# Three edits to a one-core attention and MoE kernel: where the last six output tiles are staged, how many rows eight heads' first scores contract over, and new numbers for the scheduler

## The chip, the cores and the metric

The kernel runs on one core of a Trainium2 chip (trn2). The metric is device time in microseconds (us) of one execution; a kernel's time is the median of several runs. The profile is one execution taken by the hardware profiler, and its span runs from the first to the last instruction.

## The reference

Three layers in float32, one after another. `q`, `k`, `v` are 4 x 8 x 576 x 64 (32 heads of 576 positions), `s` is 4 x 8 x 576, and `x` between the layers is 2304 x 512.

```python
def _attn_ref(q, k, v, s):
    scores = q @ k^T / sqrt(D)
    cum = np.cumsum(np.maximum(s, 0.0), axis=-1)
    bias = -(cum[:, :, :, None] - cum[:, :, None, :])
    scores = np.where(causal, -1e9, scores + np.minimum(bias, 0.0))
    attn = exp(scores - max);  attn = attn / (sum(attn) + 1e-09)
    return attn @ v

def _moe_ref(x, w1, w2, w3, w_out):      # 512 -> 1024 -> 1024 -> 512
    return ((x @ w1) * (x @ w2)) @ w3 @ w_out

def _moe2_ref(x, w_in, w_out):           # 512 -> 2048 -> 512
    h = x @ w_in
    return (h - np.tanh(h)) @ w_out
```

## The kernel before

**The stages.** (1) Attention, head by head, from 0 to about 309 us. (2) The products `x@w1` and `x@w2` and their elementwise product (`products`, matmuls at L826), mixed into the attention of later heads and going on after it. (3) `w3 @ w_out` as one matrix (L941 to L943), and the first MoE layer's output `x2` (L978 to L980). (4) The second MoE layer from about 533 us: three passes (`p`) of 768 tokens, in each eight steps (`fp`). A step forms seven matrix products per group of weights (`ws`, `x2b`, L1055), the gate `h - tanh(h)` on ACT and DVE into `gh` and `gl` (a high and a low part), and adds into six PSUM banks, each 128 tokens x 512, by three matmuls a bank and tile (L1095 to L1097). In the last step of a pass the six banks are complete; ACT copies each to SBUF and SP sends it to `out`.

**The order of the work** is made ahead of time by a list scheduler in the kernel (`Plan`). Each operation has a priority, a duration for each engine that may run it, and the buffers (or numbered parts of a buffer) that it reads and writes. The scheduler walks through modelled time and writes an instruction order for every engine; on the chip each engine keeps that order, and SP issues every DMA in its own. Priorities, and the biases by which an operation is given to ACT, DVE or POOL, come from the table `PARAM`. Where the scheduler sees PE idle in its first 66 us (`fu=66000`), it writes **dummy matmuls** (`filler`, L576) into the gap. They read a tile of zeros and nothing uses what they write. They are instructions like others: PE runs them in order whether or not work is ready.

**The first eight heads** (batch 0, `full`) compute a score tile in float32 by one matmul pair at L688 (head 0, `one`, by L686 and L695). There are five query tiles `t` of 64, 128, 128, 128 and 128 queries. The contraction has 64 rows of q and k, and five more, one for each query tile: on the query side 1 for the queries of that tile and 0 for others (`fix`), on the key side the cumulated bias relative to that tile's first position (`rel`). So the queries of tile `t` pick row 64+t. The tile `rqk` (two of them, for even and odd heads: `rqk_112` and `rqk_113` in the built program) holds both sides. Two DMAs fill its bias rows for a head: three rows for tiles 0 to 2 and two rows for tiles 3 and 4. Each score tile goes through a reduction on DVE (L705), an exponential on ACT (L711), transposes on PE against `ident` (L745), copies into `en`, and the matmul with v (L772). The first part of a `rel` row is ready only when the prefix scan over `s` is done on DVE.

**Conversions.** Weights come as 8-byte floats (`wraw`); `assemble` turns 512 columns into float32 in five steps (L515 or L516, then L517, L518, L520 and L522 on DVE), and a split into high and low parts follows. These run on ACT, DVE and POOL beside the attention.

**Output staging.** `osb_r` is a ring of two tiles of 128 x 512 (`nosb=2`). `tmp_r` is a ring of the seven tiles `cst` (three) and `asb` (four), which in stage 4 hold the step's intermediate products. In the last step of the last pass (`last`) every bank is copied in two halves of 256 columns.

```python
ob, t0, bk = osb_r.next(), p * 2 * XB + l * XB + n * P, bank[l * 3 + n]
for a, z in ((0, 256), (256, 512)) if last else ((0, 512),):
    ...
dma(lambda t0=t0: out[t0:t0 + P, :], lambda ob=ob: ob.t, P * DM * 4, [ob], [], 0)
```

Of the kernel before, what the change touches and what calls it, by code (L numbers as in the profile page):

```python
# [40 lines left out]
PARAM = dict(tail=346719, dsub2=2687.6, dcopy2=-363.2, dother2=15239, act2=-1777.4, pool2=4728.0, cs=1176.5, xs=-29.3, layw=10048, x2p=785.3, nwst=3, late=778.7,  # L41
             gate=4314.0, cst=6240.0, ramp0=1010.9, ramp1=-512.9, dsub=4382.6, dsub0=-2390.3, dcopy=-1480.1, dcopy0=-572.5, dother=1106.1, dother0=-2029.8,
             spi=2833.6, lay=0, layp=641747, layf=473733, dve0=1000.0, early=120052, raw0=0, rawp=-700.0, ng=8, nosb=2, cut=(), convq=2713.8, natb=8, nfull=8,
             wap=1402502, dve=1000.0, act=-598.5, pool=-114.4, sem=160.0, pesem=180.0, slow=1.1, convp=3444.2, npre=12, nbias=3, keep=0.5, ff=0.0, fu=66000,
             wlast=0, kbp=-210.2, qk=2491.2, kb=-1761.7, rv=-1179.0, st=83.8, fl=756.2, iv=1391.7, pv=-1105.8, ml=4388.9, bw=370.0, ntr=3, actb=1, actn=0,
             spp=3043.5, ne=2, nsb=2, ncf=5, outlag=187.2, o_qk=-577.9, o_kb=647.6, o_rv=179.7, o_iv=-2316.9, o_fl=-889.6, o_pv=-374.3, o_ml=-281.5, o_st=829.5,
             o_c0=-132.5, o_c1=211.6, o_c2=404.2, o_c3=3145.8, o_c4=-302.4, o_c5=1092.9, o_c6=-321.1, o_c7=-538.4, o_c8=-309.2, o_c9=568.4, o_c10=-644.8,
             o_c11=721.4, o_c12=620.5, o_c13=-386.2, o_c14=-1078.1, o_c15=-517.3, o_h0=-2746.5, o_h1=-2197.2, o_h2=507.3, o_h3=211.0, o_h4=-153.0, o_h5=1351.8,
             o_h6=-1038.9, o_h7=-501.6, o_h8=-600.0, o_h9=726.1, o_h10=-463.4, o_h11=308.3, o_h12=1634.4, o_h13=837.2, o_h14=-1715.4, o_h15=-171.3, o_h16=-831.4,
             o_h17=198.0, o_h18=-178.6, o_h19=1097.2, o_h20=517.6, o_h21=-1252.5, o_h22=177.5, o_h23=337.0, o_h24=-1368.9, o_h25=-531.3, o_h26=724.9, o_h27=-159.5,  # L50
             o_h28=2096.8, o_h29=-111.9, o_h30=-510.2, o_h31=-973.2)
# [289 lines left out]
def tile_kernel(ctx, tc, qk, v, s, w1, w2, w3t, w_out, w_in, w_out2, out):  # L341
# [108 lines left out]
    cst_r = abp.ring("cst", 3, [P, TB])  # L450
    asb_r = abp.ring("asb", 4, [P, TB])
# [4 lines left out]
    rqk = [att.buf(f"rqk{i}", [P, 2 * S], n=3) for i in range(2)]  # L456
# [50 lines left out]
    osb_r = p2.ring("osb", PARAM["nosb"], [P, DM], n=2)  # L507
# [90 lines left out]
    for e in e2[:1] + [None] + e2[1:]:  # L598
        if e is None:
            zero([lambda: ssum.t], [20], [ssum], -5, 1.0)  # L600
            for R in rqk:
                a = 0 if R is rqk[0] else S
                pl.op([("POOL", 1040.0 if a == 0 else 560.0, lambda R=R, a=a: nc.gpsimd.memset(R.t[D:D + 5, a:], 0.0))], w=[(R, (1, 2))], prio=-2300)
        else:
            zero([later(e, EOFF[0], EOFF[0] + D, low)], [D], [(e, 0)], -10 if e is e2[0] else 92, r=scan)
# [32 lines left out]
    def role(n, b):  # L638
        return PARAM[n] + (PARAM["o_" + n] if b == 0 else 0.0)

    def head(h, full, groups=(0, 1)):
# [32 lines left out]
        def softmax_tile(t):  # L674
            q0, q1 = QT[t]
            nq = q1 - q0
            p_ = pr + role("st", b) * t
            bi, bo = msk, (512 if nq < P else S) - q1
            pieces = [(0, q1)] if q1 <= 512 else [(0, HALF), (HALF, S)]
            for n, (k0, k1) in enumerate(pieces):  # L680
                bk = s_ring.next()

                def mm(bk=bk, k0=k0, k1=k1):
                    o_ = bk.t[:nq, :k1 - k0]
                    if one:
# [6 lines left out]
                if one:  # L692
# [3 lines left out]
                    pe(f_mm4(k1 - k0), mm, [R], [bk], p_ - 2000.0)  # L696
# [351 lines left out]
    def step(p, fp, pos, X, W):  # L1048
# [143 lines left out]
```

## Time and profile before

| what | us |
|---|---|
| median of 3 runs (lowest, highest) | 922.23 (921.72, 922.34) |
| the profiled execution, its whole time | 921.88 |
| its span | 920.2 |
| PE busy | 906.6 |
| DVE busy | 790.7 |
| ACT busy | 549.0 |
| POOL busy | 112.1 |

PE is TensorE's matmuls, DVE VectorE, ACT ScalarE, POOL GpSimd, SP the engine that issues the DMAs. Busy time of PE counts the dummy matmuls too, and it is modelled: matmuls are pipelined, so one that is listed with 0.39 us follows the one before after some 0.23 us. A window's idle time of an engine is its length less its busy time.

### The profile page before, as it was taken

Reading aid. Unit: us, or ns where it says so; the run is one execution under the profiler, and the core shown is the slowest. Engines: PE = TensorE matmul, PEld = TensorE weight load, DVE = VectorE, ACT = ScalarE, POOL = GpSimd, SP = SyncE. Lnnn points to the kernel's source line nnn. Section 1 sums busy time; section 2 is a strip of 40 time slices with the busy share of each in tenths; the row PEclk is TensorE's granted clock in tenths of the full one; section 3 lists DMA queues with packets and bytes.
Section 4 is the critical chain, followed back from the end, with each engine's and each line's share of the span. In section 5 each row is a group of like instructions: output and inputs, shape, how many; then the busy total and the mean of one; then the engine's idle time right before and its main releaser. Section 6 shows DMA issues by size and latency. Waiting matters only on the chain.

```text
span 920.2 us, 15850 instructions
## 1 busy us (share of the span) xinstructions
PE 906.6 (99%) x5174; PEld 790.6 (86%) x5174; DVE 790.7 (86%) x1884; ACT 549.0 (60%) x1292; POOL 112.1 (12%) x106
## 2 busy tenths in 40 slices
PE   9999999999999999999999989999999999999996
PEld 7777788888887888988999988989898998989885
DVE  8999999899999599989536999999998878787874
ACT  6998854343423013555446577777787667776765
POOL 1000044545442172000000000000000000000000
PEclk9999999999999999999999999999999999999998
DMA  7677766456565458898877595787977448644401
GB/s 222 202 227 194 217 203 213 130 186 212 177 220 161 154 179 279 275 296 282 270 231 236 189 306 173 255 275 236 387 236 260 116 117 304 200 116 123 115 12 69
DMA packets 102948, 189.94 MB, mean 206 GB/s; under 512 B 10594, under 2 KB 50690, under 8 KB 102867
## 3 DMA queue, kind: packets, MB, share of 16 engines
q1 hardware_dynamic: 102866, 188.94, 64.8%
q8 instruction: 41, 0.67, 0.3%
q14 instruction: 41, 0.33, 0.1%
HBM read 137.20 MB, written 48.01 MB: 201 GB/s over the span
## 4 chain that ended last, share of the span: by engine, by line
PE 89%; DVE 5%; DMA 3%; ACT 1%; issue 1%; SPq 0%; ACTq 0%; DVEq 0%
PE bank L826 21%; PE bank L1055 18%; PE bank L1096 7%; PE bank L1097 7%; PE bank L1095 7%; PE bank L745 5%; PE bank L772 5%; PE bank L979 2%; PE bank L978 2%; PE bank L980 2%; PE bank L690 2%; PE bank L688 2%; PE bank L691 2%; PE bank L941 2%; PE bank L942 2%; PE bank L943 2%
## 5 line engine op out<-in xcount | busy, mean ns | idle before, releaser
L1055 PE MATMUL bank<-x2b,ws 128*128 128x384 f32 x1008 | 192.9, 337 | 2.8 <-DMA ws<-ws_d 1.3
L1055 PEld LDWEIGHTS bank<-x2b,ws 128*128 128x128 f32 x1008 | 178.8, 188 | 12.1 <-DVE asb L1064 3.0
L711 ACT ACTIVATE e<-e,nmx 64x64 f32<-64x64 f32 (+4 forms) x160 | 89.1, 558 | 95.6 <-DVE nmx L705 95.0
L1097 PE MATMUL bank<-voh,gl 128*128 128x512 f32 x288 | 113.8, 395 | 0.0
L1096 PE MATMUL bank<-vol,gh 128*128 128x512 f32 x288 | 113.6, 394 | 0.0
L1095 PE MATMUL bank<-voh,gh 128*128 128x512 f32 x288 | 111.9, 389 | 0.0
L410 ACT ACTIVATE gh<-pg 128x384 fp32r<-128x384 f32 x96 | 50.0, 521 | 46.8 <-DVE pg L1087 46.5
L745 PE MATMUL bank<-ident,e 128*128 128x128 f32 (+1 forms) x480 | 75.4, 275 | 0.8 <-ACT e L711 0.7
L705 DVE CUSTOM_DVE_ANT_0 e<-bank,msk 64x64 f32<-64x64 f32 (+4 forms) x160 | 64.7, 420 | 4.5 <-PE bank L691 3.9
L1064 DVE TENSOR_TENSOR asb<-bank,cst 128x384 f32<-128x384 f32 x72 | 40.0, 555 | 33.2 <-PE bank L1055 32.8
L980 PE MATMUL bank<-xh,wal 128*128 128x384 f32 x192 | 64.1, 334 | 0.0
L978 PE MATMUL bank<-xh,wah 128*128 128x384 f32 x192 | 64.1, 334 | 0.0
L979 PE MATMUL bank<-xl,wah 128*128 128x384 f32 x192 | 64.1, 334 | 0.0
L1097 PEld LDWEIGHTS bank<-voh,gl 128*128 128x128 f32 x288 | 54.0, 187 | 11.5
L826 PE MATMUL bank<-xh,w2h 128*128 128x512 f32 (+1 forms) x160 | 63.3, 396 | 0.0
L745 PEld LDWEIGHTS bank<-ident,e 128*128 128x128 f32 (+1 forms) x480 | 53.8, 131 | 11.0 <-ACT e L711 2.3
L826 PE MATMUL bank<-xh,w1h 128*128 128x512 f32 (+1 forms) x160 | 63.1, 394 | 0.1
L1096 PEld LDWEIGHTS bank<-vol,gh 128*128 128x128 f32 x288 | 54.0, 187 | 9.0
L1095 PEld LDWEIGHTS bank<-voh,gh 128*128 128x128 f32 x288 | 54.1, 188 | 8.6
L515 ACT ACTIVATE wt<-wraw 128x512 f32<-128x512 f32 x62 | 41.4, 671 | 31.0 <-DMA wraw<-w3t 16.7
L826 PE MATMUL bank<-xh,w1l 128*128 128x512 f32 (+1 forms) x160 | 59.4, 371 | 0.0
L1087 DVE COPY_PREDICATED pg<-mk,th 128x384 f32<-128x384 uint32 x96 | 57.8, 602 | 1.9
(144 smaller groups left out, 2190.9 us busy)
## 6 DMA issues: line engine op xcount, KB each, us to landing
ws<-ws_d SPq DMA_DIRECT2D x168, 256.0 KB
ws_d<-wst SPq DMA_DIRECT2D x56, 256.0 KB
rqk<-qk SPq DMA_DIRECT2D x24, 576.0 KB
wraw<-w_out SPq DMA_DIRECT2D x24, 512.0 KB
x_d<-x2s SPq DMA_DIRECT2D x28, 384.0 KB
x2b<-x_d SPq DMA_DIRECT2D x14, 768.0 KB
wraw<-w SPq DMA_DIRECT2D x16, 512.0 KB
wraw<-w_in SPq DMA_DIRECT2D x16, 512.0 KB
```

What stands on the lines that cost most here:

```text
L705: nc.vector.tensor_tensor_reduce(e.t[:nq, EOFF[t] + k0:EOFF[t] + k1], bk.t[:nq, :k1 - k0], bi.t[:nq, bo + k0:bo + k1], -0.125, 3.0e38 if f ...
L711: act(lambda: nc.scalar.activation(et(), et(), AF.Exp, bias=nmx.t[:nq, i, tm:tm + 1], scale=-1.0, accum_out=ssum.t[:nq, pj, t, i:i + 1]), ...
L745: nc.tensor.transpose(bk.t[:rows, (at + m) * P:(at + m + 1) * P], e.t[:, EOFF[t] + c * P:EOFF[t] + c * P + rows], ident.t)
L826: nc.tensor.matmul(bk.t[:, :w], w_.t[:, k, f * P:(f + 1) * P], x_.t[:, k, :w], start=k == 0 and i == 0, stop=k == KC - 1 and i == 2)
L978: nc.tensor.matmul(bk.t[:, :XB], wah.t[:, f, a], ch, start=f == 0, stop=False)
L979: nc.tensor.matmul(bk.t[:, :XB], wah.t[:, f, a], cl, start=False, stop=False)
L980: nc.tensor.matmul(bk.t[:, :XB], wal.t[:, f, a], ch, start=False, stop=f == NF - 1)
L1055: nc.tensor.matmul(bk.t[:, :XB], W[i].t[:, kg, a], X[i].t[:, kg, z], start=first and kg == 0 and m == 0, stop=kg == 1 and m == 2, skip_gro ...
L1087: dve(lambda: nc.vector.copy_predicated(pg.t, mk.t.bitcast(U32), th.t), XB, [mk, th], [pg], pr, two=True)
L1095: nc.tensor.matmul(o.t, gh.t[:, a], voh[f].t, start=fp == 0 and f == fp + l * NFP, stop=False)
L1096: nc.tensor.matmul(o.t, gh.t[:, a], vol[f].t, start=False, stop=False)
L1097: nc.tensor.matmul(o.t, gl.t[:, a], voh[f].t, start=False, stop=fp == NFP - 1 and f == fp + (1 - l) * NFP)
```

## The change

The last six output tiles take the next six of the seven `tmp_r` tiles, in place of the ring of two; three of them (`l` = 0) are copied whole and three in halves. Where a full head's tile `t` is 0, 1 or 2, its scores contract over 67 rows (`D + 3`), and wait only for parts 0 to 2 of `rqk`; the two rows of tiles 3 and 4 become a part of their own (3). `cst` and `asb` tiles get two parts each, `osb` one. Every number of `PARAM` that sets an order or a choice of engine is new. Of the table one line of each is shown.

```diff
-PARAM = dict(tail=346719, dsub2=2687.6, dcopy2=-363.2, dother2=15239, act2=-1777.4, pool2=4728.0, ...
+PARAM = dict(tail=342449, dsub2=4652.6, dcopy2=-1115.7, dother2=18343, act2=-2696.6, pool2=5210.8, ...
...
-    cst_r = abp.ring("cst", 3, [P, TB])
-    asb_r = abp.ring("asb", 4, [P, TB])
+    cst_r = abp.ring("cst", 3, [P, TB], n=2)
+    asb_r = abp.ring("asb", 4, [P, TB], n=2)
...
-    rqk = [att.buf(f"rqk{i}", [P, 2 * S], n=3) for i in range(2)]
+    rqk = [att.buf(f"rqk{i}", [P, 2 * S], n=4) for i in range(2)]
...
-    osb_r = p2.ring("osb", PARAM["nosb"], [P, DM], n=2)
+    osb_r = p2.ring("osb", PARAM["nosb"], [P, DM])
...
-                    (t1 - t0) * qb * 4, [(rel, range(t0, t1))], [(R, 2)], pr + role("kb", b), issue=760.0)
+                    (t1 - t0) * qb * 4, [(rel, range(t0, t1))], [(R, 3 if t0 else 2)], pr + role("kb", b), issue=760.0)
...
+            kr, have = (D + 3, [(R, (0, 1, 2))]) if t < 3 else (D + 5, [R])
...
-                        nc.tensor.matmul(bk.t[:, :k1 - k0], rq()[:D + 5, q0:q0 + P], rk()[:D + 5, k0:k1], start=True, stop=True)
+                        nc.tensor.matmul(bk.t[:, :k1 - k0], rq()[:kr, q0:q0 + P], rk()[:kr, k0:k1], start=True, stop=True)
...
-                    pe(f_mm4(k1 - k0), mm, [R], [bk], p_)
+                    pe(f_mm4(k1 - k0), mm, have, [bk], p_)
...
-                    ob, t0, bk = osb_r.next(), p * 2 * XB + l * XB + n * P, bank[l * 3 + n]
-                    for a, z in ((0, 256), (256, 512)) if last else ((0, 512),):
+                    ob, t0, bk = (tmp_r if last else osb_r).next(), p * 2 * XB + l * XB + n * P, bank[l * 3 + n]
+                    for a, z in ((0, 256), (256, 512)) if last and l else ((0, 512),):
```

The instruction orders that come out differ on every engine. Lines below L676 have one number more after the change (L688 is L689). Three places follow.

**SP near the start.** `rqk_113` is the second head's tile, `wraw` are weights as they come, `q` and `kb_d` constants and bias rows for later heads, `rqk_112` the tile of heads 0 and 2. Before:

```order
L407 DMA rqk_113<-fix 5x576
L407 DMA wraw_85<-w 128x1024
L407 DMA wraw_114<-w 128x1024
L407 DMA rqk_113<-rel 3x1x576
L407 DMA q_125<-fix 5x576 x2
L407 DMA kb_d<-kbs 32x1728
L407 DMA q_126<-fix 5x576
L407 DMA rqk_112<-rel 3x1x576
L407 DMA rqk_112<-qk 64x1152
L407 DMA rqk_112<-fix 5x576
L407 DMA rqk_113<-rel 2x1x576
```

After:

```order
L407 DMA rqk_113<-fix 5x576
L407 DMA rqk_113<-rel 2x1x576
L407 DMA rqk_113<-rel 3x1x576
L407 DMA wraw_85<-w 128x1024
L407 DMA wraw_114<-w 128x1024
L407 DMA q_125<-fix 5x576
L407 DMA kb_d<-kbs 32x1728
L407 DMA q_125<-fix 5x576
L407 DMA rqk_112<-rel 3x1x576
```

Both bias DMAs of the second head now stand ahead of two weight loads; before, the one of two rows stood behind the third head's loads.

**PE after the first head's last score matmul (L695).** L576 are the dummies, L745 transposes of the first head's tiles, L688 (after the change L689) scores of the second head. Before, with the repeated dummies left out (8, 32 and 21 of them in the three places):

```order
L695 MATMUL bank_59<-rel,e_128 128x288
L576 LDWEIGHTS msk
L576 MATMUL bank_60<-msk 128x128
...
L745 MATMUL bank_65<-ident,e_127 128x128 x3
L745 MATMUL bank_65<-ident,e_127 64x128
...
L745 MATMUL bank_61<-ident,e_127 128x128 x3
L745 MATMUL bank_62<-ident,e_127 128x128
L745 MATMUL bank_62<-ident,e_127 64x128
...
L688 MATMUL bank_58<-rqk_113 128x64
L688 MATMUL bank_59<-rqk_113 128x192
```

After (7 and 4 dummies in two places):

```order
L696 MATMUL bank_59<-rel,e_128 128x288
L689 MATMUL bank_58<-rqk_113 128x64
L746 MATMUL bank_65<-ident,e_127 128x128 x3
L746 MATMUL bank_65<-ident,e_127 64x128
L576 LDWEIGHTS msk
L576 MATMUL bank_60<-msk 128x128
...
L689 MATMUL bank_58<-rqk_113 128x448
L689 MATMUL bank_59<-rqk_113 128x192
L746 MATMUL bank_63<-ident,e_128 64x128
```

The second head's scores moved up to the place where the dummies stood. In the whole program there are 166 dummies before and 105 after.

**ACT at the end of the program.** `bank_58` to `bank_63` are the six complete banks. Before:

```order
L410 ACTIVATE gh_5429<-pg_5445 128x384
L410 ACTIVATE osb_5447<-bank_58 128x256 x2
L410 ACTIVATE osb_5448<-bank_59 128x256 x2
L410 ACTIVATE osb_5447<-bank_60 128x256 x2
L410 ACTIVATE osb_5448<-bank_61 128x256 x2
L410 ACTIVATE osb_5447<-bank_62 128x256 x2
L410 ACTIVATE osb_5448<-bank_63 128x256 x2
```

After:

```order
L410 ACTIVATE gh_5368<-pg_5384 128x384
L410 ACTIVATE cst_100<-bank_58 128x512
L410 ACTIVATE cst_101<-bank_59 128x512
L410 ACTIVATE cst_102<-bank_60 128x512
L410 ACTIVATE asb_103<-bank_61 128x256 x2
L410 ACTIVATE asb_104<-bank_62 128x256 x2
L410 ACTIVATE asb_105<-bank_63 128x256 x2
```

All copies stay on ACT, into six different tiles.

## Rows read from the trace of the kernel before

**Rows 1.** Page: busy time by engine, and the granted clock in 40 slices
```profile
PE 906.6 (99%) x5174; PEld 790.6 (86%) x5174; DVE 790.7 (86%) x1884; ACT 549.0 (60%) x1292; POOL 112.1 (12%) x106
...
PEclk9999999999999999999999999999999999999998
```

**Rows 2.** Windows: stretch, length, busy us (instructions) by engine, clock, DMA
```profile
12.00:60.00 48.00, 48.00 (x379) 36.84 (x377) 47.81 (x160) 42.74 (x130) 0.00 (x0) 1.00 0.69 207
60.00:100.00 40.00, 38.30 (x270) 30.18 (x269) 39.22 (x116) 33.50 (x92) 0.00 (x0) 1.00 0.75 209
100.00:200.00 100.00, 100.00 (x648) 82.25 (x646) 94.55 (x280) 49.17 (x146) 40.54 (x34) 1.00 0.62 190
200.00:306.00 106.00, 106.00 (x692) 85.74 (x693) 100.93 (x296) 37.20 (x110) 42.38 (x38) 1.00 0.61 193
500.00:545.00 45.00, 42.24 (x240) 41.04 (x239) 43.54 (x88) 30.08 (x62) 0.00 (x0) 1.00 0.68 222
665.00:905.00 240.00, 240.00 (x1194) 215.88 (x1193) 195.57 (x400) 171.07 (x362) 0.00 (x0) 1.00 0.50 156
```

**Rows 3.** Waits of PE, whole span: us in total, times, longest
```profile
PE bank L1055 <- DMA ws<-ws_d: 1.3, 1, 1.3
PE bank L1055 <- DVE asb L1064: 1.1, 1, 1.1
```

**Rows 4.** Chain that ended last, 13 to 24 us: start, us, what
```profile
14.17 0.45 PE bank L576 x8
...
15.07 1.79 PE bank L576 x32
...
17.45 1.17 PE bank L576 x21
18.62 1.90 PE bank L688 x8
```

**Rows 5.** Order of time, SP's queue, 0 to 32 us: start, us, what
```profile
6.05 0.86 SPq L407 DMA_DIRECT2D wraw<-w  x2
8.77 0.77 SPq L407 DMA_DIRECT2D rqk<-rel  x1
...
15.24 1.28 SPq L407 DMA_DIRECT2D rqk<-rel  x2
```

**Rows 6.** Order of time, PE: its last matmul
```profile
912.40 0.39 PE L1097 MATMUL bank<-voh,gl 128*128 128x512 f32 x1
```

**Rows 7.** Order of time, ACT, 908 us to the end
```profile
909.42 1.34 ACT L410 ACTIVATE osb<-bank 128x256 f32<-128x256 f32 x4 [2.37 <-PE bank L1097]
912.24 1.35 ACT L410 ACTIVATE osb<-bank 128x256 f32<-128x256 f32 x4 [1.48 <-DMA out<-osb]
915.06 1.40 ACT L410 ACTIVATE osb<-bank 128x256 f32<-128x256 f32 x4 [1.46 <-DMA out<-osb]
```

**Rows 8.** Order of time, SP's queue, 908 us to the end
```profile
910.11 6.70 SPq L407 DMA_DIRECT2D out<-osb  x6
```

**Rows 9.** Chain that ended last, 900 us to the end
```profile
910.11 2.03 DMA out<-osb
```

**Rows 10.** Groups by form, DVE: two steps of a conversion, and a multiply
```profile
L522 DVE SCALAR_TENSOR_TENSOR wt<-wraw,wt 128x512 uint32<-128x512 uint32 x72 | 52.2, 726 | 0.1
L520 DVE SCALAR_TENSOR_TENSOR wt<-wraw,wt 128x512 uint32<-128x512 uint32 x72 | 50.2, 698 | 0.3
...
L800 DVE TENSOR_TENSOR xf<-xf,xr 128x512 f32<-128x512 f32 x5 | 3.4, 680 | 0.0
```

**Rows 11.** Groups by form, POOL: multiplies of the attention output
```profile
L800 POOL TENSOR_TENSOR xf<-xf,xr 128x512 f32<-128x512 f32 x11 | 14.2, 1288 | 2.0 <-DVE xf L411 2.0
```

**Rows 12.** Windows of line 522 alone (DVE), two stretches
```profile
12.00:60.00 48.00, 5.44 (x8) 1.00 0.69 207
100.00:200.00 100.00, 6.38 (x7) 1.00 0.62 190
```

**Rows 13.** Chain that ended last, whole span, one run of products
```profile
306.40 61.50 PE bank L826 x276
```

More of the change, by code (lines that the diff above doesn't have):

```diff
@@ L40 @@
 NR = D + 10
[L41 to L51, printed above, removed]
@@ new lines @@
+PARAM = dict(tail=342449, dsub2=4652.6, dcopy2=-1115.7, dother2=18343, act2=-2696.6, pool2=5210.8, cs=3667.3, xs=-1876.4, layw=10144, x2p=2814.6, nwst=3,
+             late=2630.1, gate=5266.6, cst=9284.0, ramp0=773.1, ramp1=-347.6, dsub=5509.5, dsub0=-3048.2, dcopy=-1353.0, dcopy0=-419.6, dother=975.2,
+             dother0=-2154.5, spi=2451.9, lay=0, layp=488324, layf=465259, dve0=1000.0, early=131407, raw0=0, rawp=-700.0, ng=8, nosb=2, cut=(), convq=1642.1,
+             natb=8, nfull=8, wap=2215013, dve=1000.0, act=-488.4, pool=1814.6, sem=160.0, pesem=180.0, slow=1.1, convp=4862.6, npre=12, nbias=3, keep=0.5, ff=0.0,
+             fu=66000, wlast=0, kbp=-1730.9, qk=3122.6, kb=-2784.2, rv=-528.4, st=35.8, fl=669.3, iv=1733.8, pv=-991.6, ml=3542.3, bw=370.0, ntr=3, actb=1, actn=0,
+             spp=2704.5, ne=2, nsb=2, ncf=5, outlag=174.2, o_qk=-640.2, o_kb=610.2, o_rv=246.9, o_iv=-2759.5, o_fl=-110.3, o_pv=-951.4, o_ml=72.3, o_st=652.1,
+             o_c0=-58.4, o_c1=-273.4, o_c2=774.2, o_c3=2695.0, o_c4=-94.0, o_c5=594.6, o_c6=7.3, o_c7=-279.0, o_c8=-396.0, o_c9=360.7, o_c10=-817.2, o_c11=1002.7,
+             o_c12=490.8, o_c13=-1050.8, o_c14=-1050.0, o_c15=-939.6, o_h0=-3363.9, o_h1=-2581.9, o_h2=125.2, o_h3=394.6, o_h4=-766.1, o_h5=82.4, o_h6=-1394.9,
+             o_h7=-708.0, o_h8=-871.9, o_h9=510.7, o_h10=-164.4, o_h11=-288.2, o_h12=2338.6, o_h13=484.6, o_h14=-2354.0, o_h15=-417.7, o_h16=-830.9, o_h17=140.0,
+             o_h18=274.1, o_h19=1176.2, o_h20=332.2, o_h21=-1111.0, o_h22=-260.9, o_h23=798.5, o_h24=-1600.3, o_h25=-972.7, o_h26=742.7, o_h27=585.1, o_h28=1661.0,
+             o_h29=-602.1, o_h30=-602.8, o_h31=-298.1)
@@ L602, in tile_kernel @@
                 a = 0 if R is rqk[0] else S
-                pl.op([("POOL", 1040.0 if a == 0 else 560.0, lambda R=R, a=a: nc.gpsimd.memset(R.t[D:D + 5, a:], 0.0))], w=[(R, (1, 2))], prio=-2300)
+                pl.op([("POOL", 1040.0 if a == 0 else 560.0, lambda R=R, a=a: nc.gpsimd.memset(R.t[D:D + 5, a:], 0.0))], w=[(R, (1, 2, 3))], prio=-2300)
         else:
@@ L685, in mm @@
                     if one:
-                        nc.tensor.matmul(bk.t[:, :k1 - k0], rq()[:D + 5, q0:q0 + P], rk()[:D + 5, k0:k1], start=True, stop=False)
+                        nc.tensor.matmul(bk.t[:, :k1 - k0], rq()[:kr, q0:q0 + P], rk()[:kr, k0:k1], start=True, stop=False)
                     elif full:
-                        nc.tensor.matmul(bk.t[:, :k1 - k0], rq()[:D + 5, q0:q0 + P], rk()[:D + 5, k0:k1], start=True, stop=True)
+                        nc.tensor.matmul(bk.t[:, :k1 - k0], rq()[:kr, q0:q0 + P], rk()[:kr, k0:k1], start=True, stop=True)
                     else:
@@ L695, in bias @@
                         nc.tensor.matmul(bk.t[:, :k1 - k0], sel(a), rel.t[:3 * NH, o + k0:o + k1], start=False, stop=True)
-                    pe(f_mm4(k1 - k0), mm, [R], [bk], p_ - 2000.0)
+                    pe(f_mm4(k1 - k0), mm, have, [bk], p_ - 2000.0)
                     pe(f_mm4(k1 - k0), bias, [(rel, ([0, 3, 5], [1, 4, 6], [2, 6, 7])[t % 3]), (e2[1], 4)], [bk], p_)
                 elif full:
-                    pe(f_mm4(k1 - k0), mm, [R], [bk], p_)
+                    pe(f_mm4(k1 - k0), mm, have, [bk], p_)
                 else:
@@ L1123, in step @@
                 for n in range(3):
-                    ob, t0, bk = osb_r.next(), p * 2 * XB + l * XB + n * P, bank[l * 3 + n]
-                    for a, z in ((0, 256), (256, 512)) if last else ((0, 512),):
-                        copy(lambda ob=ob, bk=bk, a=a, z=z: ob.t[:, a:z], lambda bk=bk, a=a, z=z: bk.t[:, a:z], z - a, [bk], [(ob, int(a > 0))] if last else [ob], pr, psum=True)
+                    ob, t0, bk = (tmp_r if last else osb_r).next(), p * 2 * XB + l * XB + n * P, bank[l * 3 + n]
+                    for a, z in ((0, 256), (256, 512)) if last and l else ((0, 512),):
+                        copy(lambda ob=ob, a=a, z=z: ob.t[:, a:z], lambda bk=bk, a=a, z=z: bk.t[:, a:z], z - a, [bk], [(ob, int(a > 0))] if last and l else [ob], pr, psum=True)
                     dma(lambda t0=t0: out[t0:t0 + P, :], lambda ob=ob: ob.t, P * DM * 4, [ob], [], 0)
```

## The prediction

> **What bounds the kernel now.** I read the page first: PE is busy for 906.6 of 920.2 us, at the full granted clock in every slice but the last [rows 1]. So an edit pays only where PE idles or runs something useless. The windows say where that is [rows 2]: no idle time in 12 to 60 us, 1.70 us in 60 to 100, none in 100 to 306, 2.76 in 500 to 545, none in 665 to 905. The list of PE's waits has two entries over one microsecond in its second half, on weights and on a DVE result at the start of the second MoE layer [rows 3]; the order of the work around these is the same in both programs, so I leave them as they are. Two losses remain, which these lists don't call waits. One is filled with dummies near the start, the other lies after PE's last matmul.
>
> **The opening.** In the chain that ended last, the dummies at L576 take 0.45, 1.79 and 1.17 us between 14.17 and 18.62 us, 61 of them in 3.41 us, 0.056 us each; then the second head's scores begin [rows 4]. What came so late is in SP's queue [rows 5]: the first bias DMA of the second head is issued at 8.77, but the other, of the two rows for tiles 3 and 4, is the first of a pair at 15.24. All of the head's tiles contracted over those rows, so tile 0 waited for them.
>
> The change does two things to this. Tiles 0 to 2 no longer read the two late rows. And in SP's new order both bias DMAs of that head stand right behind its constants, ahead of two weight loads. I take it that SP meets them when the bias rows are ready, as at 8.77 before, and issues both by 8.77 + 2 x 0.77 = 10.3 us. Then they land well before 14.17 if landing takes no longer than the 18.62 - 15.24 = 3.4 us that bounds the late one from above: 10.3 + 3.4 = 13.7. So the new PE order, with a score matmul where the first eight dummies stood, should find its data there. It has 11 dummies in this stretch instead of 61, and 25 later on where 36 stood: 166 - 105 = 61 fewer at 0.056 us, **3.4 us**.
>
> What hides nothing and what might: the queue behind SP's wait for the bias rows now holds the weight loads that were issued from 6.05 us [rows 5], so these go some 10.3 - 6.05 = 4.2 us later, and with them two conversions on ACT and DVE. DVE is busy for 47.81 of 48 us in 12 to 60 [rows 2]. If DVE set the pace there, filling PE's hole would win nothing; the gain has to come from DVE doing other work first. The orders show that it does: ahead of the last score reduction of the second head, DVE's order holds two finished conversions before (L522) and one after, and ahead of that of the eighth head nine and eight. A conversion's two costliest steps alone are 0.726 and 0.698 us [rows 10]; with the two shorter steps and the split it is near the size of the hole. It is put off, into a part where DVE has 5.45 and 5.07 us to spare (100 to 200 and 200 to 306) and PE no idle time. I take the whole 3.4 us; the bounds are 0, if the conversion is missed again before 100 us, and 5.1, if the 1.70 us of idle time in 60 to 100 goes too.
>
> The 67 rows are free by themselves: the same number of columns streams through PE, and only the wait is gone. Nothing in the trace prices a matmul by its rows, so I put 0 with a bound of 0 either way; the row counts of other score matmuls aren't needed for the sum.
>
> **The tail.** PE's last matmul starts at 912.40 and takes 0.39 us: the last bank is complete at 912.79 [rows 6]. Banks follow each other by three matmuls, 0.68 us: 909.39, 910.07, 910.75, 911.43, 912.11, 912.79. ACT copies the first two tiles as they come, then waits 1.48 and 1.46 us for a DMA to free a staging tile, and ends its last copy at 915.06 + 1.40 = 916.46 [rows 7]; SP's six issues are over right behind it, at 910.11 + 6.70 = 916.81 [rows 8]. With six tiles neither wait is there. A tile's copy in two halves is 1.34 / 2 = 0.67 us, which just keeps pace with the banks; whole tiles are no dearer. The last copy then runs from 912.81 to 912.81 + 0.70 = 913.51. Everything behind the last copy, 920.2 - 916.46 = 3.74 us, moves up with it: 916.46 - 913.51 = **2.95 us**.
>
> The end is safe if six transfers in a row are no slower than two. A tile of 256 KB takes 2.03 us to land when two are in flight [rows 9], and the second, issued some 0.7 us after the first, had landed by 912.9, since the four copies that begin at 912.24 run without a gap [rows 7]. I take 2.9. If each transfer needed 0.95 us of the queue's time instead of 0.68, the sixth would be 5 x 0.27 = 1.4 us late and the gain 1.6; that is the lower bound. The copies' targets are free in time: `cst` and `asb` tiles are last read by gate operations ahead of the last `gh`, and ACT has been done with that for 2.37 us when it starts to copy at 909.42 [rows 7].
>
> **The rest of the numbers.** The attention is drawn together: 504 of the 960 product matmuls stand ahead of the last attention matmul before, 456 after. Multiplies of the attention output (L800) go from POOL to DVE: of 32 of each size DVE did ten in all, and does 31; POOL had 22 and keeps one. Ten gate operations of the last stage go from DVE to POOL, which was idle there. All this costs nothing on PE as long as DVE keeps some slack: 44.43 of 240 us in 665 to 905, 10.52 of 206 in 100 to 306 [rows 2]. I take 0; the upper bound is the price of the slower rival below, and the lower one is in the opening's 5.1.
>
> **Sum**, against the profiled execution's own 921.88 us: 921.88 - 3.4 - 2.9 = 915.6. The median of the runs is 0.35 above that execution, so I forecast **915.9**.
>
> **Rivals.**
>
> *The opening gives its gain back.* The put-off conversions are missed when the products need their weights, and PE waits in 60 to 100 us, where it idles already and DVE has 0.78 us left [rows 2]. Against it: the put-off work is one conversion and most of what PE does there is not products. The time is that of the tail alone, 922.23 - 2.9 = 919.3.
>
> *DVE becomes the bound in the attention, and the kernel slower.* Eleven more multiplies of 0.680 us [rows 10] and ten small ones are some 9.6 us more of DVE; those on POOL took 1.288 us each [rows 11], so they were taken off an engine that had room. And 48 fewer products, at 61.50 / 276 = 0.22 us each [rows 13], stand in the stretch, so DVE has 10.7 us less time for the attention. Together that is 20 us against 11.3 us of slack in 60 to 306. What speaks against it: the order also takes work off DVE in that stretch, 13 copies into `en`, four into `xf`, four into `asb`, five weight casts and four conversions, which makes up for most. If it did not, PE would wait for some 9 us: 915.9 + 9 = 925. It decides from 6.3 + 1.8 = 8.1 us of new waits on.
>
> POOL's work also slows DVE's beside it: L522 takes 5.44 / 8 = 0.68 us with POOL idle, 6.38 / 7 = 0.91 in 100 to 200 us where POOL is busy for 40% [rows 12, 2]. The Trainium skill (GPSIMD Engine Reference, 1. Specifications) states that the two share their memory interfaces, so that instructions with two inputs contend; this row agrees. By that rule the multiplies taken from POOL cost DVE less than 9.6 us, and the ten gate operations given to POOL lengthen some on DVE in the last stage, where the slack above covers it.
>
> *The start goes cold.* If the second head's rows land later than 14.17 us, PE now stands idle where it ran dummies. The granted clock has been full in every early slice [rows 1]; at 1.2 instead of 2.4 GHz, the 10 us of matmuls from 14 to 24 us would take up to 10 us more, and the kernel would be at 919 or, with the wait, 925. The Trainium skill (TensorE: Matmul & The Clock Gate, Part 1) states that an idle PE falls back to the lower clock. No row here shows a fall before the last slice.
>
> *More than forecast.* The new order also closes the 1.70 us of 60 to 100 us and part of the 2.76 us of 500 to 545: 912 to 914.
>
> *The edits do little.* DMAs pile up at the end and the second head still waits: 921 to 923.
>
> **How the numbers follow.** A measurement of this kernel can tell about 0.2%, 1.84 us, from no change. Both gains as summed: 0.52 (914 to 917.5). Opening given back in part or whole: 0.24 (917.5 to 920.4, with a sixth of it just above 920.4). More than forecast: 0.11. Little: 0.07. DVE the bound: 0.04, cold start: 0.02. Faster: 0.52 + 0.20 + 0.11 = 0.83; within 0.2%: 0.07 + 0.04 = 0.11; slower: 0.06. The range for 8 in 10 leaves out the two slower cases, the case without effect and the far end of the gains: 913.3 to 919.8.
>
> **What would show it.** In the new profile: 105 dummies; the second head's first score matmul at about 14.2 us and no wait of PE ahead of it; ACT without a wait on a DMA after 909, its last copy ending 0.7 us after PE's last matmul; 3.7 us from there to the end of the span; no new entry over one microsecond in PE's waits between 60 and 310 us; DVE's idle time in 100 to 306 above zero. I am wrong if PE's waits in 60 to 306 grow by more than 2 us, if the sixth output DMA lands over 3 us after its issue, or if PE idles for the second head.

## The result, and the profile after

| | before | after |
|---|---|---|
| median, us (lowest, highest; 4 runs each) | 922.15 (921.72, 922.34) | 913.69 (913.06, 915.92) |
| span of the profiled execution, us | 920.2 | 911.0 |
| first product matmul (L826, after L827), us | 63.3 | 59.3 |
| first x2 matmul (L978, after L979), us | 433.0 | 428.1 |
| second MoE layer, first matmul (L1055, after L1056), us | 532.8 | 528.0 |
| its first output matmul (L1095, after L1096), us | 547.0 | 541.5 |
| last matmul starts, us | 912.40 | 906.79 |

The ratio is 0.9913 (95% interval 0.9895 to 0.9931): faster by 0.9%, with 913.69 inside the forecast range and 2.2 us below the forecast.

The table is read downwards, by how far ahead the new kernel is. It is 4.0 us ahead at the first product, 4.9 at x2, 4.8 at the second layer, 5.5 at that layer's first output and 5.6 at PE's last matmul. The spans differ by 9.2 us, so 3.6 us came behind the last matmul.

The page's line of busy time and its granted clock, as in [rows 1]:

```profile
PE 903.4 (99%) x5113; PEld 787.2 (86%) x5113; DVE 788.9 (87%) x1879; ACT 555.0 (61%) x1311; POOL 98.0 (11%) x89
...
PEclk9999999999999999999999999999999999999999
```

PE has 61 matmuls fewer, the dummies, and 3.2 us less busy time. The windows (columns as in [rows 2]) show that its idle time shrank too: 0.74 us in 60 to 100 and 1.69 in 500 to 545, where 1.70 and 2.76 stood. DVE has 10.7 us to spare in 100 to 306.

```profile
12.00:60.00 48.00, 47.89 (x349) 35.77 (x348) 47.72 (x161) 44.83 (x137) 0.00 (x0) 1.00 0.80 225
60.00:100.00 40.00, 39.26 (x276) 30.95 (x275) 39.64 (x124) 34.51 (x101) 0.00 (x0) 1.00 0.66 207
100.00:200.00 100.00, 100.00 (x659) 82.12 (x658) 95.08 (x287) 55.77 (x161) 24.83 (x20) 1.00 0.67 214
200.00:306.00 106.00, 106.00 (x666) 86.43 (x665) 100.21 (x291) 33.19 (x101) 34.02 (x30) 1.00 0.56 172
500.00:545.00 45.00, 43.31 (x240) 41.24 (x239) 43.81 (x90) 30.52 (x63) 0.00 (x0) 1.00 0.71 238
```

In the list of PE's waits the 1.3 us on a weight load of [rows 3] is gone in this execution (the seventh run below, with the same order, has 1.1 us of it):

```profile
PE bank L1056 <- DVE asb L1065: 1.1, 1, 1.1
PE bank L576 <- DVE msk L572: 1.1, 1, 1.1
PE bank L691 <- DVE nmx L706: 0.5, 1, 0.5
PE bank L1056 <- DVE wt L517: 0.5, 1, 0.5
```

The chain near the start answers to [rows 4]. The second head's first score matmul starts at 13.44, not 18.62, and 11 dummies stand in the stretch:

```profile
13.44 0.17 PE bank L689 x2
...
14.29 0.39 PE bank L576 x7
...
14.70 1.35 PE bank L689 x4
...
16.16 0.22 PE bank L576 x4
```

SP's queue answers to [rows 5]: both bias DMAs of the second head go out from 7.49 on, and the weight loads follow them.

```profile
7.49 1.48 SPq L407 DMA_DIRECT2D rqk<-rel  x2
9.03 0.88 SPq L407 DMA_DIRECT2D wraw<-w  x2
```

Part of the 4.0 us is no effect of the change. The load of `rel`, from which the first head's bias is made, is issued at 1.72 us in both kernels, but it landed earlier in the profile of after. DVE's first operation on it, before and after:

```profile
5.07 0.45 DVE L588 TENSOR_SCALAR rel<-rel 32x576 f32<-32x576 f32 x1 [1.83 <-DMA rel<-s]
```

```profile
3.97 0.45 DVE L588 TENSOR_SCALAR rel<-rel 32x576 f32<-32x576 f32 x1 [0.73 <-DMA rel<-s]
```

The first head's last bias matmul starts at 12.95 us, not 13.69. In the first run below, which opens in the order of before, that operation starts at 4.07 and the first product at 63.0; in the fifth and seventh, which open in the order of after, the first product starts at 59.6 and 59.8. So the lead at the first product is 3.2 to 4.0 us.

The tail answers to [rows 6 to 8]: PE's last matmul, then ACT's copies, then SP's issues, in three views. No copy waits for a DMA any more.

```profile
906.79 0.39 PE L1098 MATMUL bank<-voh,gl 128*128 128x512 f32 x1
```

```profile
903.82 1.96 ACT L410 ACTIVATE cst<-bank 128x512 f32<-128x512 f32 x3 [1.69 <-PE bank L1098]
905.86 2.02 ACT L410 ACTIVATE asb<-bank 128x256 f32<-128x256 f32 x6
```

```profile
904.44 1.69 SPq L407 DMA_DIRECT2D out<-cst  x3
906.54 1.69 SPq L407 DMA_DIRECT2D out<-asb  x3
```

The last copy ends at 905.86 + 2.02 = 907.88, which is 0.70 us behind the last complete bank (906.79 + 0.39 = 907.18), as forecast. From there to the end are 3.12 us; before they were 3.74.

### The profile page after: what moved, and what is told of

The parts are those of the page before. It is cut to its first block, busy times and chain, and to the rows that moved or that the text cites. A ratio compares the mean times of both kernels' runs of the same rounds, so it can differ in the third digit from the quotient of the medians.

```text
span 911.0 us, 15741 instructions
## 1 busy us (share of the span) xinstructions
PE 903.4 (99%) x5113; PEld 787.2 (86%) x5113; DVE 788.9 (87%) x1879; ACT 555.0 (61%) x1311; POOL 98.0 (11%) x89
## 4 chain that ended last, share of the span: by engine, by line
PE 92%; DVE 5%; DMA 1%; issue 1%; ACT 1%; SPq 0%; ACTq 0%; DVEq 0%
PE bank L827 22%; PE bank L1056 19%; PE bank L1097 7%; PE bank L1098 7%; PE bank L1096 7%; PE bank L746 6%; PE bank L773 5%; PE bank L979 2%; PE bank L980 2%; PE bank L981 2%; PE bank L691 2%; PE bank L689 2%; PE bank L692 2%; PE bank L942 2%; PE bank L943 2%; PE bank L944 2%
## 5 line engine op out<-in xcount | busy, mean ns | idle before, releaser
L1056 PE MATMUL bank<-x2b,ws 128*128 128x384 f32 x1008 | 193.0, 337 | 1.7 <-DVE asb L1065 1.1
L1056 PEld LDWEIGHTS bank<-x2b,ws 128*128 128x128 f32 x1008 | 178.7, 188 | 11.3 <-DVE asb L1065 1.5
L712 ACT ACTIVATE e<-e,nmx 128x576 f32<-128x576 f32 (+4 forms) x160 | 89.0, 557 | 84.0 <-DVE nmx L706 82.4
L1096 PE MATMUL bank<-voh,gh 128*128 128x512 f32 x288 | 111.9, 389 | 0.0
L410 ACT ACTIVATE wst<-wf 128x256 fp32r<-128x256 f32 x55 | 22.1, 413 | 76.4 <-PE bank L827 41.1
L979 PE MATMUL bank<-xh,wah 128*128 128x384 f32 x192 | 64.1, 334 | 0.0
L827 PE MATMUL bank<-xh,w1h 128*128 128x512 f32 (+1 forms) x160 | 62.7, 392 | 0.1
L827 PE MATMUL bank<-xh,w2h 128*128 128x512 f32 (+1 forms) x160 | 62.6, 391 | 0.0
L1096 PEld LDWEIGHTS bank<-voh,gh 128*128 128x128 f32 x288 | 54.1, 188 | 8.7
L827 PE MATMUL bank<-xh,w1l 128*128 128x512 f32 (+1 forms) x160 | 59.3, 371 | 0.0
```

Of the source, the lines that this page charges most:

```text
L410: pl.op([("ACT", c_act(n, psum), lambda: nc.scalar.activation(dst(), src(), AF.Copy)), ("DVE", c_dve(n, not psum), lambda: nc.vector.tenso ...
L712: act(lambda: nc.scalar.activation(et(), et(), AF.Exp, bias=nmx.t[:nq, i, tm:tm + 1], scale=-1.0, accum_out=ssum.t[:nq, pj, t, i:i + 1]), ...
L827: nc.tensor.matmul(bk.t[:, :w], w_.t[:, k, f * P:(f + 1) * P], x_.t[:, k, :w], start=k == 0 and i == 0, stop=k == KC - 1 and i == 2)
L979: nc.tensor.matmul(bk.t[:, :XB], wah.t[:, f, a], ch, start=f == 0, stop=False)
L1056: nc.tensor.matmul(bk.t[:, :XB], W[i].t[:, kg, a], X[i].t[:, kg, z], start=first and kg == 0 and m == 0, stop=kg == 1 and m == 2, skip_gro ...
L1096: nc.tensor.matmul(o.t, gh.t[:, a], voh[f].t, start=fp == 0 and f == fp + l * NFP, stop=False)
```

## The experiments

A first theory was that of the prediction: the opening and the tail add up, and the table of numbers by itself is worth nothing. Its rivals were that the buffer part, not the 67 rows, frees the opening, and that the edits depend on the numbers. The edits were therefore run alone, left out one at a time, and together on the old numbers. "Part" below means both the part of its own for the two late rows and the 67 rows; each result has the ratio to the kernel before with its interval.

| | neither | tail alone | part alone | tail and part |
|---|---|---|---|---|
| old numbers | before | 0.9969 (first run) | 1.0060 (third) | 1.0043 (ninth) |
| new numbers | 1.0109 (fourth) | 1.0076 (sixth) | 0.9967 (fifth) | 0.9913 (after) |

**First run: the tail alone.**

```diff
...
-                    ob, t0, bk = osb_r.next(), p * 2 * XB + l * XB + n * P, bank[l * 3 + n]
-                    for a, z in ((0, 256), (256, 512)) if last else ((0, 512),):
+                    ob, t0, bk = (tmp_r if last else osb_r).next(), p * 2 * XB + l * XB + n * P, bank[l * 3 + n]
+                    for a, z in ((0, 256), (256, 512)) if last and l else ((0, 512),):
...
```

> The kernel before with the last six tiles in the seven temporaries, and nothing else; its instruction order differs from before in those twelve copies and DMAs alone. Theory (the two waits for a staging tile were the whole loss of the tail, and six transfers in flight queue no worse than two): 2.9 to 3.6 us faster than before, near 918.9, span 7.41 us behind the last matmul's end shrinking to about 4. Rival (the six transfers pile up): 1.6 us or less, 920.5 or more, and the stretch from the last copy to the end longer than 3.74 us.

Measured: 918.85 us (918.11 to 919.48), ratio 0.9969 (0.9958 to 0.9981), 2.9 us below the 921.74 of before in the same job. All instruction orders are those of before except the tail's rows on ACT and SP. So the tail term is shown by itself, at the forecast's size.

**Second run: the part of its own, with 69 rows and the wait on all parts kept; third run: the same with 67 rows.** Old numbers and old tail in both. The second:

```diff
-    rqk = [att.buf(f"rqk{i}", [P, 2 * S], n=3) for i in range(2)]
+    rqk = [att.buf(f"rqk{i}", [P, 2 * S], n=4) for i in range(2)]
...
-                    (t1 - t0) * qb * 4, [(rel, range(t0, t1))], [(R, 2)], pr + role("kb", b), issue=760.0)
+                    (t1 - t0) * qb * 4, [(rel, range(t0, t1))], [(R, 3 if t0 else 2)], pr + role("kb", b), issue=760.0)
```

> The kernel before with one thing changed: the two late bias rows are a part of rqk of their own (3), so the two bias DMAs of a head no longer write the same part; all tiles still contract over 69 rows and wait for every part. Its order has 100 dummy matmuls in place of 166. Theory (the second DMA was held back only because both wrote one part, and the 67 rows do nothing): as fast as e3, 3.4 to 4.9 us faster than before, near 918. Rival 1 (the tiles must stop waiting for the late rows, so the 67 rows carry the gain): PE waits for the second head's rows at about 14 us, and the time stays within 1 us of before. Rival 2 (the opening gives its gain back to put-off conversions): within 1 us of before too, but with the waits of PE later, in 60 to 100 us.

The third adds:

```diff
+            kr, have = (D + 3, [(R, (0, 1, 2))]) if t < 3 else (D + 5, [R])
...
-                        nc.tensor.matmul(bk.t[:, :k1 - k0], rq()[:D + 5, q0:q0 + P], rk()[:D + 5, k0:k1], start=True, stop=True)
+                        nc.tensor.matmul(bk.t[:, :k1 - k0], rq()[:kr, q0:q0 + P], rk()[:kr, k0:k1], start=True, stop=True)
```

> The kernel before with the own part and the 67 rows for tiles 0 to 2, old numbers, old staging. Its instruction order is that of e2 on every engine. Theory: 3.4 to 4.9 us faster than before, near 918, and equal to e2 within 0.7 us. Rival (67 rows matter): over 1 us faster than e2.

Measured: 927.11 (926.52 to 927.54), ratio 1.0058 (1.0045 to 1.0072), and 926.75 (925.31 to 928.75), ratio 1.0060 (1.0046 to 1.0073). The two are alike, with the same instruction orders and 100 dummies each, and both miss what was expected. The two-row DMA stands right behind the other in both, issued from 7.49 us as in after. So the part of its own makes the opening, and neither the 67 rows nor the shorter list of waits adds to it. Yet both kernels are slower than before. The first product starts at 58.0 in both, 5.3 us ahead of before, and x2 at 430.0 and 429.7, 3.0 and 3.3 ahead. The first of these leads counts a little too high, since six of the matmuls with v that stand ahead of the first product before come after it here. The rest of the drop from 5.3 to some 3 us comes without more idle time of PE (1.6 us in 60 to 430 in the third run, 1.7 before); what causes it is not shown. Behind x2 the whole lead goes: in the third run the last matmul starts at 915.9, 3.5 us behind before. PE's longest waits in the third run:

```profile
PE bank L1056 <- DMA ws<-ws_d: 2.1, 1, 2.1
PE bank L1056 <- ACT xd L410: 1.9, 2, 1.2
PE bank L980 <- DVE xl L414: 1.5, 1, 1.5
PE bank L1056 <- DVE asb L1065: 1.5, 1, 1.5
```

These waits lie between 490 and 550 us, where the second layer starts.

**Fourth run: the new numbers alone.**

```diff
-PARAM = dict(tail=346719, dsub2=2687.6, dcopy2=-363.2, dother2=15239, act2=-1777.4, pool2=4728.0, ...
+PARAM = dict(tail=342449, dsub2=4652.6, dcopy2=-1115.7, dother2=18343, act2=-2696.6, pool2=5210.8, ...
```

> The kernel before with the new numbers alone. Its order has 170 dummy matmuls and the second bias DMA of the second head as late as before. Theory (the numbers close small waits and no more): within 1.5 us of before, 920.7 to 923, with the hole at 14 to 18 us as before. Rival (the numbers carry the opening's gain): 3 us or more faster.

Measured: 931.59 (931.17 to 932.30), ratio 1.0109 (1.0096 to 1.0123), far outside what was expected. It has 170 dummies, and the first product starts at 63.3 as before. SP issues the two-row DMA in a pair at 15.04 us, behind a third head's loads, as in [rows 5]:

```profile
8.39 0.77 SPq L407 DMA_DIRECT2D rqk<-rel  x1
...
15.04 1.28 SPq L407 DMA_DIRECT2D rqk<-rel  x2
```

So the numbers do not move that DMA; without the part they cost 9.85 us, of which 3.9 are there at x2 (436.9) and 7.9 at the second layer (540.7).

**Fifth, sixth and seventh run: the changed kernel with one edit taken back.** The fifth has the old tail (the first run's diff reversed), the sixth the old part and 69 rows (those of the second and third reversed), the seventh 69 rows and the wait on all parts, but the part of its own (the third's reversed).

> The changed kernel with the ring of two tiles and six copies in halves put back; new numbers and the own part stay. Theory (the tail is worth the same whatever stands ahead of it, 2.9 us as the run of the tail alone had it): 916.6. Rival (the tail's edit shifts the schedule ahead of it too): outside 915.6 to 917.6.

> The changed kernel with one shared part for all bias rows and 69 rows everywhere; new numbers and new staging stay; 170 dummy matmuls. Theory (the new numbers fit only the order that comes out with the own part): as slow as the numbers alone less the tail, 931.6 - 2.9 = 928.7. Rival (the numbers alone were unlucky in one wait): 920 or less.

> The changed kernel with 69 rows and waits on every part for tiles 0 to 2; the late rows keep their own part. Its instruction order is that of the changed kernel on every engine. Theory (the 67 rows are worth nothing; the own part is what let the second DMA go): equal to the changed kernel within 0.7 us, 913 to 914.5, second head's first score matmul before 14.5 us. Rival (the waits count): PE waits for the late rows at 13.5 us and the time is 1 us or more above.

Measured: 918.28 (916.63 to 922.56, 12 runs), ratio 0.9967 (0.9953 to 0.9981); 928.82 (927.05 to 930.38), ratio 1.0076 (1.0062 to 1.0089); 914.35 (913.88 to 915.42), ratio 0.9922 (0.9910 to 0.9934). The seventh has after's order on every engine, and its interval overlaps after's: the 67 rows are worth nothing that can be measured. The sixth came out as expected: with the new numbers the part is worth 15 us, with the old ones it costs 5 (7 with the tail in). The fifth missed its 916.6: it is 4.6 us above after, and its runs lie 5.9 us apart. In its profile the last bank is complete at 909.99 and the span ends at 916.8, 6.8 us later, where after needs 3.8, so the tail itself gives 3.0. PE's order is the same as after's, but its last matmul was 2.8 us later in this execution. Most of that is in two waits for DMAs, 0.8 us for `q<-qs` in 60 to 100 us and 2.1 for `ws<-ws_d` at the start of the second layer; why these landed later with the same order stays open. Part of the spread of its times goes with the granted clock: 922.56 us came with a mean of 0.994, 916.69 with 0.999.

**Eighth run: the changed kernel with one number 18 ns off.**

```diff
-             natb=8, nfull=8, wap=2215013, dve=1000.0, act=-488.4, pool=1814.6, ...
+             natb=8, nfull=8, wap=2215013, dve=1000.0, act=-470.0, pool=1814.6, ...
```

> The changed kernel with one number moved by 18 ns (act, -488.4 to -470.0), which sets when the scheduler gives work to ACT; 127 dummies and another order from the first microseconds on. Theory (what the numbers are worth is how well one order happens to fit, above all where the second layer starts, and any other order gives several us away): 916 to 926, with new waits of PE at 430 to 560 us. Rival (the numbers moved work for good, and a nearby set keeps it): 913 to 915.

Measured: 925.01 (921.76 to 929.17, 12 runs), ratio 1.0038 (1.0025 to 1.0052), 11 us above after, though tail and part are both in. The first product is early (58.9); PE waits at the same places as in the third run, 2.0 us on xd, 2.0 on xl and 1.5 on ws. So a kernel with tail, part and nearly the same numbers is slower than before: what the numbers are worth belongs to the one order that they make. Only this one step away from them was run.

**Ninth run: part and tail on the old numbers; tenth run: the same with new numbers for the second layer only.** The ninth joins the diffs of the first three runs. The tenth adds to it new numbers for what leads up to the second layer and for that layer (two lines of the table are shown; `layp`, `layf` and `wap` are new too, the attention's numbers stay as before):

```diff
-PARAM = dict(tail=346719, dsub2=2687.6, dcopy2=-363.2, dother2=15239, act2=-1777.4, pool2=4728.0, cs=1176.5, xs=-29.3, layw=10048, x2p=785.3, nwst=3, late=778.7,
-             gate=4314.0, ...
+PARAM = dict(tail=342449, dsub2=4652.6, dcopy2=-1115.7, dother2=18343, act2=-2696.6, pool2=5210.8, cs=3667.3, xs=-1876.4, layw=10144, x2p=2814.6, nwst=3, late=2630.1,
+             gate=5266.6, ...
```

> The own part with 67 rows, and the six staging tiles, with every number of the table as before. Theory (the edits add up, and the own part needs numbers that fit it): the 926.75 us of the own part alone less the 2.9 us that the tail was worth alone, 923.9 us; the loss lies at 430 to 560 us. Rival 1 (the own part and the tail are worth their sum of the forecast, 3.4 and 2.9 us, whatever the numbers): 915.9 us. Rival 2 (the tail is worth more when the end is reached in another order): under 922 us.

> As the run with own part, 67 rows and six staging tiles on the old numbers, but the numbers that only set the second MoE layer and what leads up to it (tail, late, gate, layp, layf, wap, x2p and the like) are those of after; the attention's numbers stay old. Theory (the own part's gain is handed back at the start of the second MoE layer, and the numbers of that layer keep it): some 916 us, the waits on xd and ws at 530 to 555 us gone. Rival (the attention's numbers decide how early the work reaches 430 us, so the old ones lose it whatever comes later): 920 us or more.

Measured: 925.62 (924.23 to 927.96), ratio 1.0043 (1.0031 to 1.0056), and 917.55 (917.31 to 920.01), ratio 0.9964 (0.9951 to 0.9977). PE's orders of the two are identical up to the end of the x2 matmuls, and x2 starts at 431.4 and 431.1. From there to the last matmul the tenth gains 7.8 us. Windows of the ninth, x2 to second layer and second layer to its first output:

```profile
431.40:535.00 103.60, 100.63 (x578) 99.67 (x576) 67.82 (x142) 53.31 (x119) 0.00 (x0) 1.00 0.71 230
535.00:552.40 17.40, 11.95 (x54) 10.79 (x55) 16.30 (x33) 13.39 (x28) 0.00 (x0) 0.90 0.88 318
```

The same of the tenth, 3.8 and 4.1 us shorter, the second with 2.3 us of idle time of PE in place of 5.5 and at the full clock:

```profile
431.10:530.90 99.80, 99.80 (x577) 99.80 (x576) 66.22 (x138) 54.09 (x119) 0.00 (x0) 1.00 0.73 239
530.90:544.20 13.30, 11.03 (x63) 10.42 (x62) 11.85 (x25) 10.26 (x22) 0.00 (x0) 1.00 0.92 307
```

Together PE idles for 8.4 us in the ninth and 2.3 in the tenth, and a clock of 0.90 over 17.4 us makes some 1.7 more. PE's waits in the ninth are 3.2 us on `ws`, 2.0 on `xd` (tiles that take x2 on its way to memory, `xf_d`), 1.5 on `asb` and 1.5 on `xl`; the tenth has 1.6 on `ws` and 0.7 on `asb`. SP's queue shows how those on `ws` and `xd` come about. In the ninth, four loads of `w_out` take it from 523.67 to 533.33, copies of xd follow to 537.26, and the first of the thirteen `ws` loads that come close together goes out at 539.32:

```profile
523.67 9.66 SPq L407 DMA_DIRECT2D wraw<-w_out  x4
533.42 3.84 SPq L407 DMA_DIRECT2D xf_d<-xd  x3
...
539.32 1.93 SPq L407 DMA_DIRECT2D ws<-ws_d  x4
...
543.05 5.91 SPq L407 DMA_DIRECT2D ws<-ws_d  x9
```

In the list of waits of that queue from 515 to 552 us, the longest is on conversions, which free the tile that the next load of `w_out` goes to:

```profile
SPq L407 <- DVE wt L522: 12.9, 7, 4.3
```

It is 5.4 us in after. But together with the waits on another step of the conversions (L517) it is 14.7 us in the ninth, 12.1 in after and 10.1 in the tenth, so these waits are only a little longer; what differs more is how many loads of `w_out` stand ahead of the `ws` loads. In after and in the tenth the `ws` loads start at 530.60 and 532.18:

```profile
530.60 1.38 SPq L407 DMA_DIRECT2D ws<-ws_d  x3
```

```profile
532.18 2.40 SPq L407 DMA_DIRECT2D ws<-ws_d  x3
```

There are 24 loads of `w_out`. Ahead of these `ws` loads stand 22 of them in the second, third and ninth run, 23 in the fourth and sixth and 24 in the eighth; in before, after and all other runs it is 21. Those six need 116.7 to 121.6 us from the first x2 matmul to the second layer's first output, the other eight 113.1 to 114.6. So the opening's gain is lost again where the second layer's weights stand in SP's order behind more loads that wait for conversions, and the late-stage numbers decide that order. This is read from the traces; no run moves these loads alone, and the wait on `xl`, at 508 us, lies ahead of them. The ninth is 1.7 us above what was expected and the tenth 1.5, so the edits do not add up exactly; the tenth is 3.9 us above after, and 3.0 of these are there at x2: the attention's numbers are worth the rest.

**Eleventh and twelfth run: the kernels before and after without the dummies behind the 69th** (97 of 166 and 36 of 105; the rest of the order is kept).

```diff
+    n_fill = [0]
...
+        n_fill[0] += 1
+        if n_fill[0] > 69:
+            return
```

> The kernel of before, with the order of all other work kept word for word, and the dummy matmuls behind the 69th (97 of 166) not issued. Theory (the second head's data are late, and the dummies fill a wait that is there anyway): within 1 us of before, PE idle between 14 and 19 us, clock full. Rival 1 (the dummies themselves hold the scores back): 1 to 3 us faster. Rival 2 (PE falls to the lower clock while it idles): slower by up to 10 us, the granted clock of 12 to 30 us below 1.

> The changed kernel, with the order of all other work kept, and the dummy matmuls behind the 69th (36 of 105) not issued. Theory (the 36 left fill gaps in which the next transposes or scores are not ready): within 1 us of after, 912.7 to 914.7 us, clock full. Rival 1 (they cost what they last, 36 x 0.056 us): 911.7 us. Rival 2 (the clock falls): slower, the granted clock of 12 to 30 us below 1.

Measured: 925.99 (924.84 to 926.13), ratio 1.0042 (1.0030 to 1.0054), 4.3 us slower than before; and 915.30 (913.32 to 916.61), ratio 0.9931 (0.9918 to 0.9944), which overlaps after's interval, with a span of 911.2 beside 911.0. The theory fell for the eleventh: the dummies do more than fill a wait. The second head's first scores in order of time before, and PE in the eleventh (L692 are scores, L749 transposes in this kernel):

```profile
18.45 2.06 PE L688 MATMUL bank<-rqk 69*128 69x64 f32 x8
```

```profile
13.97 0.66 PE L749 MATMUL bank<-ident,e 128*128 128x128 f32 x4 [0.19 <-ACT e L715]
16.36 0.77 PE L749 MATMUL bank<-ident,e 128*128 128x128 f32 x5 [1.74 <-ACT e L715]
17.54 1.32 PE L692 MATMUL bank<-rqk 69*128 69x64 f32 x6 [0.42 <-DMA rqk<-rel]
19.14 1.86 PE L692 MATMUL bank<-rqk 69*128 69x448 f32 x2 [0.27 <-DVE nmx L709]
```

The scores start 0.9 us sooner than before, at 17.54 (0.4 of it because the first head was earlier in this execution, its last bias matmul at 13.13 and not 13.52), and what they waited for last is the late bias DMA. But the windows of the same kernel show the granted clock at 0.70 in 18 to 20 us, then at 0.50, the lower level of 1.2 GHz, and full again only from 30 us on:

```profile
18.00:20.00 2.00, 1.73 (x5) 0.86 (x5) 2.00 (x8) 0.72 (x3) 0.00 (x0) 0.70 0.77 284
20.00:22.00 2.00, 2.00 (x6) 1.10 (x5) 1.35 (x5) 1.54 (x7) 0.00 (x0) 0.50 0.99 346
...
28.00:30.00 2.00, 2.00 (x11) 1.19 (x8) 1.59 (x4) 1.06 (x5) 0.00 (x0) 0.74 0.00 0
30.00:32.00 2.00, 2.00 (x15) 1.64 (x14) 1.82 (x8) 1.79 (x7) 0.00 (x0) 1.00 0.76 236
```

From 18 to 30 us the share of the clock not granted is 0.6 + 4.0 + 0.5 = 5.1 us. Less the 0.9 us won, that is 4.2; the first product starts 4.1 us later than before, at 67.4. In the twelfth PE idles for 0.42 us at the place of the first dummies, and the clock stays full:

```profile
15.00 1.35 PE L693 MATMUL bank<-rqk 69*128 69x448 f32 x4 [0.42 <-DVE nmx L710]
```

## Why the prediction was right, and where it was not

**The bound and the sum.** PE was the bound, and both losses named were paid back: 4.0 us by the first product where 3.4 was forecast, 3.6 behind the last matmul where 2.9 was. The forecast was 2.2 us too high. By the profiles (9.2 us against 6.3) it missed 0.6 us ahead of the first product and 0.7 in the tail, nearly all of it scatter of the two executions, and 1.6 us in between. The last is the rival "more than forecast", and the time fell into its 912 to 914 us. In 60 to 100 us its mechanism shows: PE idles for 0.74 us in after and in the seventh run (1.54 in the fifth, with the wait of 0.8), for 1.70 before and 1.73 in the first run, which has the order of before there. In 500 to 545 it shows in part: 1.69 us in after but 2.28 in the seventh run, 2.76 before but 2.31 in the first, so at least half of the 1.1 us there is within scatter.

**The tail**, point by point: the copies keep pace with the banks, the last one ends 0.70 us after the last bank, and six transfers in a row are no slower than two. The first run gave 2.9 us alone. In the changed kernel's profile it was 3.6, since the last copy's DMA ended after 3.12 us and not 3.74; in the first run's profile that stretch is 3.7, so 0.6 of it is scatter of single executions and no part of the edit. Over all profiles the stretch is 3.1 to 3.9 us with the old tail and 3.1 to 3.7 with the new one, while the span ends 6.9 to 7.6 us behind the last bank in the six with the old tail and 3.8 to 4.4 in the eight with the new one. One of the signs of being wrong, a sixth DMA that lands over 3 us after its issue, can't be read, as no row has the landing: its issue starts at 907.90 us, and the span ends 3.1 us later (3.7 before).

**The opening** has the right size (3.2 to 4.0 us, forecast 3.4) and half of the cause wrong. The prediction credited the release of tiles 0 to 2 from the late rows together with SP's new order, and did not say which edit makes that order. The second, third and seventh run show that contracting 67 rows and waiting for fewer parts do nothing that can be measured, and the fourth that the numbers don't move the DMA. The part of its own does: before, both bias DMAs of a head wrote the same part, and the scheduler put the second far behind; with two parts it puts it next to the first. That the shared part held it back as a second write to the same buffer is read from the code's bookkeeping, while the runs show only that the part decides. That putting off conversions is harmless in the attention was right for the changed kernel: no new wait over one microsecond there, and DVE with 10.7 us to spare.

**"The rest of the numbers" at 0** is the step that failed. The prediction read it as a term beside the others. It is none: the new numbers cost 9.85 us alone, and with part and tail in place they are worth 11.9 (925.62 less 913.69). What they do is keep the opening's gain. Without them the rival *the opening gives its gain back* happens, not in 60 to 100 us as it was put but for the most part at 490 to 550, with SP's queue as the likely reason; and it gives back more than it won. Its price of 919.3 was too low for that: the ninth run is at 925.62. The prediction had looked at that place and left it out, since the order of the work around those waits is the same in both programs; it is not when only some of the change is made.

**The cold start** did not happen, as forecast: the first score came at 13.44 us, not 14.2, and no idle time replaced the dummies. The eleventh run puts its price, in the old order, at 4.3 us in the whole time. The rule of the Trainium skill (TensorE: Matmul & The Clock Gate, Part 1) that an idle PE falls back to the lower clock is seen there, with a granted clock of 0.50 in 20 to 28 us.

**DVE as the bound** did not come about: 4.92 and 5.79 us of idle time in 100 to 200 and 200 to 306. (The multiplies at L800 are 16 of each of two sizes, 32 in all, and not 32 of each; the prices were worked out with the right counts.)

## What to carry to other kernels

An edit and the scheduler's numbers that were fitted to it are one change: run each with the other's old state before crediting either. Where a late buffer holds up an in-order queue, look at how finely its writes are declared as well as at how much is read. Dummies in front of late data may hold the clock up; take them away only together with the wait that they fill.

## What the runs showed of the hardware

The clock was dearer than the theory of the eleventh run had it. After idle times of 0.19, 1.74, 0.42 and 0.27 us between 13.8 and 19.2 us it fell to 0.50, and stayed there until past 28 us although the records list PE as busy from 20 on; that cost 4 us net. A single gap of 0.42 us in the twelfth run left it full. In the ninth run PE idled for 1.53 us and then for 3.23; behind the second wait the granted clock was 0.50 in 549 to 552 us, and twelve matmuls took 3.88 us where the twelve before them took 2.36:

```profile
543.12 2.36 PE L1056 MATMUL bank<-x2b,ws 128*128 128x384 f32 x12 [1.53 <-DVE asb L1065]
548.71 3.88 PE L1056 MATMUL bank<-x2b,ws 128*128 128x384 f32 x12 [3.23 <-DMA ws<-ws_d]
```

A load from memory that was issued at the same 1.72 us in each kernel, that of `rel`, let DVE start at 3.97 us in one profile and at 5.07 in another.
